# Broadcast means moved behind a slot's scores, first gated blocks and gates moved ahead, more idle products at the start

## The chip, the cores and the metric

The kernel runs on one core of one Trainium2 chip. The time is that of the device, in microseconds, for one execution; the median over runs counts. Five engines work side by side, each through its own instructions in order: TensorE (PE in the rows), VectorE (DVE), ScalarE (ACT), GpSimd (POOL), and SyncE (SP), which here only issues DMAs. They wait for each other by semaphores.

## The reference

Three layers, all in float32. Block-sparse attention over 2 batches, 8 heads, 768 positions of width 64; a mixture of 4 experts on the 1536 tokens of width 512; a gated MLP. Cut to what matters here:

```python
# attention, per batch and head; blocks of 32 positions, window 16
k_sum = k.reshape(nb, 32, D).max(1);  v_sum = v.reshape(nb, 32, D).mean(1)
scores = concat([where(|i-j| < 16, scale * q @ k.T, -1e9), scale * q @ k_sum.T + log(32)])
a = exp(scores - max);  a = a / (a.sum(-1) + 1e-9)
x = a @ concat([v, v_sum])
# experts
p = domain_probs / (domain_probs.sum(-1) + 1e-9)
x = sum(p[:, e:e+1] * (relu(x @ w1[e]) @ w2[e]) for e in range(4))
# last layer
h = x @ w_in;  out = (h * sigmoid(1.702 * h)) @ w_out
```

## The kernel before

**Precision.** Most products run with each float32 operand cut in two fp32r parts, high and low, as three matmuls (high by high, high by low, low by high). `split` makes such parts of a weight block: ACT casts the high part, DVE or POOL subtracts it from the raw block to get the low part. `hidden` and `low` do the same for activations.

**Attention in slots.** Two heads at a time (a head pair, `hp`, 4 per batch) and 4 windows of 64 queries make a group, named in the program by batch, head pair and first window (`010` is batch 0, pair 1, window 0). There are 24 groups: batch 0's twelve first, then batch 1's. The work is a pipeline written out by hand, one slot per group and a few behind them. Slot i holds, in the order in which each engine gets it: `att_a(i)`, then products of the first expert layer or idle products on TensorE, then `att_b(i)`.

- `att_a(i)`: `scores` of group i (16 small matmuls into PSUM bank 5, then on DVE the mask `s` and the row maximum `nm`); `normalise` of group i-1 (two short DVE instructions `sm`, a POOL product over `s`); `windows` of group i+2 (DVE and POOL copies into `kw`); the weight splits that the table `middle` names for the slot; in slots 0 to 3 and 12 to 15, where a new head pair begins, `fold_v` on POOL (half of a block sum of v), and in the slot behind each, `sums` on DVE (the other half, into `vsum`).
- `att_b(i)`: `transposes` of group i-2 (PE into bank 6, ACT copies to `aT`); `values` of group i-3 (PE into bank 7, tile `xo`; ACT casts to `xh`, and `low` later subtracts on DVE to `xl`); then `means` of group i-2; `exponentials` of group i on ACT; and what the table `after` names for the slot, mostly loads.
- `means(g)`: with the first group of a head pair, PE transposes `vsum` into a bank of its own name `pvs` (bank 4 in batch 0, bank 5 in batch 1) and ACT scales it into `vm`; for every group, POOL then copies `vm` to the last 24 rows of the group's v tile (`v_home` or `vw`). `values` of the next slot reads them.

**The start.** Loads are issued by SP in one order: keys, queries, v and weights of the first groups. 10 idle 128 by 128 products (`warm`, written by `spin`) run ahead of the first scores. Slots 0 to 3 have no other dense work; the list `SPIN` puts 0, 4, 4, 4 idle products into them behind the scores. Slots 4 to 7 hold `early(k)`: 12 products each, the part of head pair k of the first four hidden blocks (units 0 to 3, in banks 0 to 3).

**First expert layer.** A unit is 128 hidden channels by 256 or 512 tokens of batch 0. `first(i)` computes a unit's hidden block into a bank; `hidden(i)` makes it relu times gate on DVE (`gated`, tile `g`, which reads the broadcast gates `pb`), casts it on ACT, and puts the low part on the list `pending`, which `flush` empties on DVE. `second(i)` multiplies by the second weight into banks 0 to 3, the banks of units 0 to 3. So `second(0)` can write banks 2 and 3 only when the gated blocks 2 and 3 have been read. From slot 8 on, slots are interleaved with units: unit 4 has slots 8 and 9, unit 5 has 10 and 11, and so on (unit 8 has three, 16 to 18). In the kernel before, `hidden_blocks(0, 1)` stands behind slot 8 and `hidden_blocks(2, 3, 4)` behind slot 9, each with the low parts of the block before it in between, and `second(0)`, `second(1)` follow.

**Gates.** `gates_load` brings the probabilities (48 numbers per partition) after the loads of v; `gates`, behind slot 4, sums, adds, inverts and multiplies on DVE (four instructions), then stores them to DRAM; behind slot 5 `load_p(0, 0)` reads them back, broadcast to all partitions, as `pb`.

After the attention slots the rest of the program works through pairs of hidden blocks of the other experts and the last layer, 44 pairs, TensorE nearly always busy.

## Time and profile before

| | |
|---|---|
| median of 3 runs | 865.87 us (865.2 to 867.35) |
| the profiled execution's own time | 866.81 us |
| its span, first to last instruction | 865.0 us |
| mean granted TensorE clock | 0.993 |
| TensorE busy | 830.1 us, 96% |
| DVE, ACT, POOL busy | 602.0, 397.1, 479.6 us |
| slots 0 to 3 on TensorE | to 22.95 us (scores of slot 4) |
| slots 4 to 7 | 22.95 to 39.97 us |
| slots 8 to 18 | 39.97 to 96.97 us |

Times of instructions are counted from the span's start. A line of a list of waits tells how long an engine stood still before instructions of one line, how often, and whose work ended the wait. The granted clock is 1.00 where TensorE had its full 2.4 GHz and 0.50 where it had 1.2 GHz.

### The profile page before, as it was taken

What the parts mean: (1) busy time and instruction counts of PE and PEld (TensorE: products, weight loads), DVE (VectorE), ACT (ScalarE), POOL (GpSimd) and SP (SyncE); (2) the same over time, 40 slices, a digit from 0 to 9 for tenths busy, and PEclk for the clock granted to TensorE, in tenths of its full rate; (3) what the DMA queues carried; (4) which work ended last, traced back from release to release, by engine and by line L of the source; (5) the groups of instructions that cost most, each with busy time, mean ns of one, the idle gap of its engine ahead of it and who ended that gap; (6) DMA issues with size and microseconds to landing.
All of it is one profiled execution on the core that took longest, in us unless ns stands there. A gap on an engine that the chain in (4) does not pass through costs nothing.

```text
span 865.0 us, 13668 instructions
## 1 busy us (share of the span) xinstructions
PE 830.1 (96%) x5068; PEld 748.7 (87%) x5068; DVE 602.0 (70%) x899; ACT 397.1 (46%) x914; POOL 479.6 (55%) x416
## 2 busy tenths in 40 slices
PE   6978999999999999989999999999899999999998
PEld 5866778899999989889989998999788998998896
DVE  7677538879999884688788688897788753432332
ACT  4766742535444444233333334446556453434442
POOL 6657435656667674265564657867478642323221
PEclk9899999999999999999999999999999999999999
DMA  9853412366767536386776874223534627653422
GB/s 284 255 174 87 138 38 103 117 249 244 266 218 264 207 149 259 114 314 231 277 252 251 287 276 143 77 73 110 183 134 169 232 110 280 207 193 112 150 93 74
DMA packets 48371, 159.93 MB, mean 185 GB/s; under 512 B 5424, under 2 KB 8752, under 8 KB 43184
## 3 DMA queue, kind: packets, MB, share of 16 engines
q1 hardware_dynamic: 48304, 159.06, 53.3%
q8 instruction: 40, 0.66, 0.3%
q14 instruction: 27, 0.22, 0.1%
HBM read 110.78 MB, written 48.26 MB: 184 GB/s over the span
## 4 chain that ended last, share of the span: by engine, by line
PE 72%; DVE 14%; DMA 6%; issue 4%; ACT 2%; POOL 2%; SPq 0%; DVEq 0%; POOLq 0%; ACTq 0%
PE o L782 19%; PE Y L664 17%; PE o L807 13%; PE X L664 5%; PE h L387 3%; DVE S L547 3%; PE o L418 2%; DMA wA<-kept 2%; DVE hid L337 2%; PE sc L231 2%; DVE g L716 2%; PE xo L282 1%; DVE x L452 1%; DMA q<-kq 1%; DVE g L709 1%
## 5 line engine op out<-in xcount | busy, mean ns | idle before, releaser
L782 PE MATMUL o<-hid,wB 128*128 128x512 f32 x1344 | 261.3, 336 | 3.5 <-DVE y L799 2.3
L782 PEld LDWEIGHTS o<-hid,wB 128*128 128x128 f32 x1344 | 214.6, 188 | 25.4 <-DVE y L799 3.0
L576 POOL TENSOR_TENSOR wB<-rawB,wB 128x512 fp32r<-128x512 f32 x88 | 124.9, 1429 | 136.8 <-ACT wB L575 122.0
L807 PE MATMUL o<-wB,hid 128*128 128x512 f32 x576 | 147.8, 393 | 0.0
L711 ACT CAST hid<-g 128x384 fp32r<-128x384 f32 x176 | 90.7, 516 | 117.8 <-DVE g L701 82.4
L337 DVE TENSOR_TENSOR hid<-g,hid 128x384 fp32r<-128x384 f32 (+2 forms) x152 | 129.3, 858 | 19.1 <-ACT hid L711 13.6
L807 PEld LDWEIGHTS o<-wB,hid 128*128 128x128 f32 x576 | 106.9, 188 | 17.0
L552 POOL TENSOR_TENSOR wA<-S,wA 128x512 fp32r<-128x512 f32 x48 | 70.3, 1465 | 45.5 <-ACT wA L551 30.1
L701 DVE SCALAR_TENSOR_TENSOR g<-g,pb 128x384 f32<-128x384 f32 x84 | 83.3, 991 | 2.0
L552 POOL TENSOR_TENSOR wA<-rawA,wA 128x512 fp32r<-128x512 f32 (+1 forms) x48 | 59.7, 1243 | 42.0 <-ACT wA L551 36.4
L664 PE MATMUL Y<-xh,wA 128*128 128x384 f32 x224 | 66.2, 336 | 4.3 <-DMA wA<-kept 2.8
L664 PE MATMUL Y<-xt,wA 128*128 128x384 f32 x336 | 67.5, 335 | 1.7 <-ACT prq L724 1.5
L337 POOL TENSOR_TENSOR hid<-g,hid 128x384 fp32r<-128x384 f32 x40 | 45.6, 1141 | 30.0 <-ACT hid L711 30.0
L724 ACT COPY prq<-Y 128x384 f32<-128x384 f32 x44 | 21.2, 481 | 85.0 <-PE Y L664 68.7
L664 PEld LDWEIGHTS Y<-xt,wA 128*128 128x128 f32 x336 | 56.0, 188 | 4.7 <-ACT prq L724 2.0
L716 DVE TENSOR_TENSOR g<-X,prq 128x384 f32<-128x384 f32 x44 | 24.4, 555 | 43.0 <-PE X L664 40.3
L575 ACT CAST wB<-rawB 128x512 fp32r<-128x512 f32 x88 | 52.5, 619 | 1.4 <-DMA rawB<-wts 1.4
L261 POOL TENSOR_TENSOR s<-s,sm 128x480 f32<-128x480 f32 x24 | 28.3, 1180 | 40.9 <-DVE sm L260 38.5
L708 ACT ACTIVATE sg<-g 128x384 f32<-128x384 f32 x48 | 25.3, 527 | 55.9 <-DVE g L716 55.7
L709 DVE TENSOR_TENSOR g<-g,sg 128x384 f32<-128x384 f32 x48 | 34.2, 713 | 21.5 <-ACT sg L708 19.9
L664 PEld LDWEIGHTS Y<-xh,wA 128*128 128x128 f32 x224 | 41.2, 188 | 7.4 <-DVE arena L605 2.7
L615 POOL TENSOR_SCALAR arena<-arena 128x512 int32<-128x512 int32 x32 | 25.4, 792 | 39.6 <-DVE arena L611 39.6
(451 smaller groups left out, 1633.2 us busy)
## 6 DMA issues: line engine op xcount, KB each, us to landing
kept<-wA SPq DMA_DIRECT2D x20, 1792.0 KB, 6.7
wA<-kept SPq DMA_DIRECT2D x20, 1792.0 KB, 8.7
arena<-w SPq DMA_DIRECT2D x32, 512.0 KB, 4.9
rawB<-wts SPq DMA_DIRECT2D x28, 512.0 KB, 4.0
rawA<-wts SPq DMA_DIRECT2D x16, 512.0 KB, 7.8
w<-arena SPq DMA_DIRECT2D x32, 256.0 KB, 2.5
rawB<-w SPq DMA_DIRECT2D x16, 512.0 KB, 4.3
rawA<-w SPq DMA_DIRECT2D x8, 512.0 KB, 8.0
```

Source lines behind the costliest of these rows:

```text
L261: nc.gpsimd.tensor_tensor(out=s, in0=s, in1=sm.unsqueeze(2).to_broadcast([P, GW, KA]), op=ALU.mult)
L337: engine.tensor_tensor(out=hl, in0=g, in1=hh.bitcast(F32), op=ALU.subtract)
L552: nc.gpsimd.tensor_tensor(out=lo, in0=x, in1=hi.bitcast(F32), op=ALU.subtract)
L575: nc.scalar.copy(hi, rawB[j][:, f])
L576: nc.gpsimd.tensor_tensor(out=lo, in0=rawB[j][:, f], in1=hi.bitcast(F32), op=ALU.subtract)
L664: nc.tensor.matmul(ps[:, 0:HS], ws[w], xs[x][:, k], start=(fresh and k == 0 and m == 0), stop=(k == 1 and m == 2), skip_group_check=True,)
L701: nc.vector.scalar_tensor_tensor(out=g, in0=g, scalar=0.0, in1=pbs[ph, s][:, tok], op0=ALU.max, op1=ALU.mult)
L709: nc.vector.tensor_tensor(out=g, in0=c, in1=sg, op=ALU.mult)
L711: heads.append(lambda: nc.scalar.copy(hh, g))
L716: nc.vector.tensor_tensor(out=g, in0=ps, in1=x, op=ALU.add)
L782: nc.tensor.matmul(o, wB[j][:, w, f, c], tiles[f][:, x, t], start=fr, stop=last, skip_group_check=True,)
L807: nc.tensor.matmul(o, tiles[f][:, x, c], wB[j][:, w, f], start=(new and f == 1 and m == 0), stop=(old and f == 0 and m == 2),)
```

## The change

- **Means.** `means` of group i-2 moves from `att_b` behind `values` to `att_a` straight behind `scores`. The transpose of `vsum` no longer has a bank of its own name: it goes into columns 256 to 383 of the newest `xo` tile in bank 7 (in slot 2 into a fresh one). The next `values` takes a new tile in bank 7 and so comes after ACT's read of the transpose.
- **Gates.** Their load becomes the third load of the program. The sum is made on POOL in slot 0 (`gates_sum`, three short instructions); the inverse (DVE), the product (POOL) and the store come in slot 1, and the broadcast load in slot 4 in place of 5.
- **Gated blocks.** Blocks 0 and 1 come straight behind slot 7, blocks 2 and 3 straight behind slot 8, block 4 behind slot 9; the low parts come with the next slot's `flush`.
- **Idle products.** `SPIN` becomes 4, 8, 4, 4, and 4 more stand ahead of `values` in slots 2 and 3.
- **Split 2.** In slot 3 its low part moves from POOL to DVE, behind split 3.
- **Loads.** The queries of group 4 are issued ahead of the last v loads of batch 0.

```diff
--- before.py
+++ after.py
@@ -210,13 +210,17 @@
             axis=AX.X, op=ALU.add,
         )
 
+    xo = {}
+
     def means(g):
         b, hp, w0 = g
         if (b, hp) not in vms:
             vms[b, hp] = att.tile([P, P], F32, tag="vm", bufs=4, name=f"vm{b}{hp}")
-            ps = bank(5 if b else 4, f"pvs{b}{hp}")
-            nc.tensor.transpose(ps[0:KA, 0:P], vsum[hp % 2], ident)
-            nc.scalar.mul(vms[b, hp][KW:KA], ps[KW:KA, 0:P], 1.0 / BLK)
+            if "ps" not in xo:
+                xo["ps"] = bank(7, "xo")
+            ps = xo["ps"][:, GQ : GQ + P]
+            nc.tensor.transpose(ps[0:KA], vsum[hp % 2], ident)
+            nc.scalar.mul(vms[b, hp][KW:KA], ps[KW:KA], 1.0 / BLK)
         nc.gpsimd.tensor_copy(
             vs[g][KW:KA], vms[b, hp][KW:KA].unsqueeze(1).to_broadcast([NB, GW, P])
         )
@@ -276,7 +280,7 @@
         b, hp, w0 = g
         a = st.pop(g)
         v = vs.pop(g)
-        ps = bank(7, f"xo{b}{hp}{w0}")
+        ps = xo["ps"] = bank(7, f"xo{b}{hp}{w0}")
         for j in range(GW):
             for h in range(2):
                 nc.tensor.matmul(
@@ -308,13 +312,21 @@
     def gates_load():
         nc.sync.dma_start(out=dp, in_=dpT.rearrange("e (p c) -> p e c", c=NC))
 
+    ds = const.tile([P, NE // 2 + 1, NC], F32, name="ds")
+
+    def gates_sum():
+        two, one = ds[:, 0 : NE // 2], ds[:, NE // 2]
+        nc.gpsimd.tensor_tensor(out=two, in0=dp[:, 0 : NE // 2], in1=dp[:, NE // 2 :], op=ALU.add)
+        nc.gpsimd.tensor_tensor(out=one, in0=two[:, 0], in1=two[:, 1], op=ALU.add)
+        nc.gpsimd.tensor_scalar(
+            out=one, in0=one, scalar1=1.0, scalar2=1e-9, op0=ALU.mult, op1=ALU.add
+        )
+
     def gates():
-        ds = const.tile([P, NC], F32, name="ds")
-        nc.vector.tensor_reduce(out=ds, in_=dp.rearrange("p e c -> p c e"), axis=AX.X, op=ALU.add)
-        nc.vector.tensor_scalar(out=ds, in0=ds, scalar1=1e-9, scalar2=None, op0=ALU.add)
-        nc.vector.reciprocal(out=ds, in_=ds)
-        nc.vector.tensor_tensor(
-            out=dp, in0=dp, in1=ds.unsqueeze(1).to_broadcast([P, NE, NC]), op=ALU.mult
+        one = ds[:, NE // 2]
+        nc.vector.reciprocal(out=one, in_=one)
+        nc.gpsimd.tensor_tensor(
+            out=dp, in0=dp, in1=one.unsqueeze(1).to_broadcast([P, NE, NC]), op=ALU.mult
         )
         nc.sync.dma_start(out=pscr.rearrange("e (p c) -> p e c", c=NC), in_=dp)
 
@@ -842,6 +854,8 @@
     def att_a(i):
         if i < NG:
             scores(groups[i])
+        if 2 <= i < NG + 2:
+            means(groups[i - 2])
 
         if 1 <= i < HP - 1:
             maxima(*groups[i + 1][:2])
@@ -860,10 +874,9 @@
     def att_b(i):
         if 2 <= i < NG + 2:
             transposes(groups[i - 2])
+        spin(SPIN_MORE.get(i, 0))
         if 3 <= i < NG + 3:
             values(groups[i - 3])
-        if 2 <= i < NG + 2:
-            means(groups[i - 2])
         if i < NG:
             exponentials(groups[i])
         if 3 <= i < NG + 3:
@@ -876,7 +889,7 @@
     pool, dve = nc.gpsimd, nc.vector
     middle = {
         2: [lambda: split(0, A, pool), lambda: split(1, A, dve)],
-        3: [lambda: split(2, A, pool), lambda: split(3, A, dve)],
+        3: [lambda: split(3, A, dve), lambda: split(2, A, dve)],
         5: [lambda: split(0, C, pool)],
         6: [lambda: split(1, C, pool)],
         7: [lambda: split(4, A, dve)],
@@ -896,7 +909,9 @@
     def x_whole():
         xf[1] = slot("xf", [P, KC, S], F32, "x1")
 
-    after = {0: [x_parts], 4: [gates], 5: [lambda: load_p(0, 0)], 8: [x_whole]}
+    after = {
+        0: [x_parts, gates_sum], 1: [gates], 4: [lambda: load_p(0, 0)], 8: [x_whole],
+    }
 
     def later(i, *acts):
         after.setdefault(i, []).extend(acts)
@@ -919,6 +934,8 @@
     for hp in range(HP):
         load_k(0, hp)
         load_q(groups[hp])
+        if hp == 0:
+            gates_load()
         if hp in (1, 2):
             load_vt(0, hp - 1)
             load_v(groups[hp - 1])
@@ -928,10 +945,9 @@
     load_v(groups[2])
     load_w(2, A)
     load_w(3, A)
+    load_q(groups[4])
     load_vt(0, 3)
     load_v(groups[3])
-    gates_load()
-    load_q(groups[4])
     load_v(groups[4])
     load_q(groups[5])
 
@@ -947,7 +963,8 @@
         maxima(0, hp)
         windows(groups[hp])
     START = 4 + KC
-    SPIN = (0, 4, 4, 4)
+    SPIN = (4, 8, 4, 4)
+    SPIN_MORE = {2: 4, 3: 4}
     for i in range(START):
         att_a(i)
         if i < len(SPIN):
@@ -956,15 +973,8 @@
             early(i - len(SPIN))
         att_b(i)
 
-
-    def hidden_blocks(*blocks):
-        for i in blocks:
-            before = list(pending)
-            pending.clear()
-            hidden(i)
-            for act in before:
-                act()
-
+    for i in range(2):
+        hidden(i)
     sl = START
     LAST = NG + 3
     steps = []
@@ -994,12 +1004,13 @@
         n = SLOTS.get(i, 2)
         one_slot()
         if i == EARLY:
-            hidden_blocks(0, 1)
+            for k in range(2, EARLY):
+                hidden(k)
         first(i)
         for _ in range(n - 1):
             one_slot()
         if i == EARLY:
-            hidden_blocks(2, 3, 4)
+            hidden(i)
         if sl == LAST:
             flush()
         if i < EARLY + 2:
```

**PE, slot 3 to the head of slot 4, before** (`sc` scores, `at` transposes, `xo` values, `pvs` the transpose for the means, `h` a hidden block):

```order
L231 MATMUL sc030_279<-kw030_239,q030_129 64x120 x8
L943 MATMUL warm_146<-ident_68 128x128 x4
L269 MATMUL at010_308<-ident_68,s010_199 120x128 x4
L282 MATMUL xo000_315<-aT000_263,v_home0_91 64x64 x8
L218 MATMUL pvs01_326<-ident_68,vsum1_104 120x128
L231 MATMUL sc004_345<-kw004_245,q004_140 64x120 x8
L387 MATMUL h0_365<-xh0_186,w0A0_98 128x256
```

The same place after:

```order
L235 MATMUL sc030_298<-kw030_259,q030_131 64x120 x8
L222 MATMUL xo_253<-ident_68,vsum1_104 120x128
L959 MATMUL warm_147<-ident_68 128x128 x4
L273 MATMUL at010_331<-ident_68,s010_207 120x128 x4
L959 MATMUL warm_147<-ident_68 128x128 x4
L286 MATMUL xo000_342<-aT000_283,v_home0_91 64x64 x8
L235 MATMUL sc004_367<-kw004_265,q004_139 64x120 x8
L222 MATMUL xo000_342<-ident_68,vsum0_103 120x128
L399 MATMUL h0_391<-xh0_191,w0A0_98 128x256
```

The transpose of `vsum` now stands ahead of the slot's transposes and values instead of behind them, and four more idle products stand ahead of the values.

**DVE, from slot 8's last instructions to slot 10's mask, before** (`g` a gated block, `hid` its low part, `ks` block maxima, `xl` the low part of the attention's output):

```order
L168 TENSOR_TENSOR w0A1_99<-raw_b_97,w0A1_99 128x512
L337 TENSOR_TENSOR hid0_663<-g_667,hid0_663 128x256
L297 TENSOR_TENSOR xl0_187<-xo024_713,xh0_186 128x256
L187 TENSOR_REDUCE ks10_730<-k10_545 128x24
L331 SCALAR_TENSOR_TENSOR g_741<-h2_373,pb00_480 128x256
L331 SCALAR_TENSOR_TENSOR g_744<-h3_377,pb00_480 128x256
L337 TENSOR_TENSOR hid2_740<-g_741,hid2_740 128x256
L331 SCALAR_TENSOR_TENSOR g_749<-h4_671,pb00_480 128x256
L337 TENSOR_TENSOR hid2_740<-g_744,hid2_740 128x256
L239 SCALAR_TENSOR_TENSOR s028_790<-sc028_781,mask_73 128x480
```

The gated blocks 2 and 3 (`h2`, `h3`) after:

```order
L343 SCALAR_TENSOR_TENSOR g_629<-h1_395,pb00_430 128x256
L243 SCALAR_TENSOR_TENSOR s008_641<-sc008_632,mask_73 128x480
L248 TENSOR_REDUCE nm008_643<-s008_641 128x4
L263 TENSOR_SCALAR sm034_612<-sm034_612 128x4
L264 RECIPROCAL sm034_612<-sm034_612 128x4
L199 COPY kw028_649<-k02_124 128x4x96
L349 TENSOR_TENSOR hid0_625<-g_626,hid0_625 128x256
L349 TENSOR_TENSOR hid0_625<-g_629,hid0_625 128x256
L301 TENSOR_TENSOR xl0_192<-xo014_663,xh0_191 128x256
L343 SCALAR_TENSOR_TENSOR g_687<-h2_399,pb00_430 128x256
L343 SCALAR_TENSOR_TENSOR g_690<-h3_403,pb00_430 128x256
L243 SCALAR_TENSOR_TENSOR s018_715<-sc018_706,mask_73 128x480
```

The gated blocks 2 and 3 stood at the end of slot 9, behind its split, low part and block maxima; they now stand at the end of slot 8, ahead of slot 9's mask (`s018`), and blocks 0 and 1 ahead of slot 8's.

**POOL, slot 13, before** (`s` normalise, `kw` windows, `w0ex` a split, `vT` a fold, `vw` the copy of the means):

```order
L261 TENSOR_TENSOR s100_940<-s100_940,sm100_969 128x480
L200 COPY kw130_1016<-ks13_975 128x4x24
L168 TENSOR_TENSOR w0ex_102<-raw_b_97,w0ex_102 128x512
L181 TENSOR_TENSOR vT11_833<-vT11_833 128x24x16
L220 COPY vw038_831<-vm03_469 24x512
```

The same slot after:

```order
L224 COPY vw038_845<-vm03_449 24x512
L265 TENSOR_TENSOR s100_954<-s100_954,sm100_983 128x480
L200 COPY kw130_1031<-ks13_989 128x4x24
L168 TENSOR_TENSOR w0ex_102<-raw_b_97,w0ex_102 128x512
L181 TENSOR_TENSOR vT11_847<-vT11_847 128x24x16
```

The copy of the means went from the slot's last place on POOL to its first.

## Rows read from the trace of the kernel before

**Rows 1.** The page: span; busy time, share and instructions of each engine.

```profile
span 865.0 us, 13668 instructions
...
PE 830.1 (96%) x5068; PEld 748.7 (87%) x5068; DVE 602.0 (70%) x899; ACT 397.1 (46%) x914; POOL 479.6 (55%) x416
```

**Rows 2.** Stretches: length, busy PE, PEld, DVE, ACT, POOL, granted clock, DMA, GB/s.

```profile
0.00:28.00 28.00, 19.92 (x168) 17.49 (x170) 18.35 (x38) 12.16 (x42) 18.61 (x33) 0.88 0.98 298
...
40.00:73.00 33.00, 27.89 (x320) 24.14 (x320) 25.48 (x59) 22.51 (x84) 18.83 (x24) 0.95 0.60 182
73.00:96.00 23.00, 18.29 (x225) 14.71 (x222) 14.79 (x35) 14.64 (x53) 16.15 (x21) 1.00 0.31 90
96.00:126.00 30.00, 29.99 (x291) 23.77 (x292) 13.39 (x31) 17.66 (x68) 13.12 (x19) 1.00 0.27 86
126.00:160.00 34.00, 32.27 (x173) 26.70 (x170) 24.99 (x27) 12.52 (x23) 14.36 (x9) 1.00 0.20 70
```

**Rows 3.** Waits of PE, 0 to 160 us: total, times, longest.

```profile
PE xo L282 <- POOL vw L220: 5.9, 8, 1.9
PE o L418 <- DVE g L331: 3.0, 1, 3.0
...
PE xo L282 <- POOL v_home L220: 2.3, 1, 2.3
...
PE sc L231 <- DMA q<-kq: 0.7, 1, 0.7
```

**Rows 4.** Two single microseconds, columns as in rows 2.

```profile
22.00:23.00 1.00, 0.30 (x3) 0.08 (x3) 0.42 (x1) 0.95 (x5) 1.00 (x3) 0.50 1.04 363
...
53.00:54.00 1.00, 1.00 (x6) 1.00 (x6) 0.00 (x0) 0.01 (x1) 0.00 (x0) 0.50 0.00 0
```

**Rows 5.** The chain that ended last: start, us, what, instructions.

```profile
22.95 1.87 PE sc L231 x16
24.82 2.72 PE h L387 x12
...
28.85 0.97 PE sc L231 x16
29.81 1.63 PE h L387 x12
...
50.75 3.91 PE o L418 x18
...
61.66 3.07 PE o L418 x24
```

**Rows 6.** PE in order of time, slot 1: four idle products.

```profile
9.21 1.16 PE L943 MATMUL warm<-ident 128*128 128x128 f32 x8
```

**Rows 7.** DVE in order of time: start, us, what, idle before and releaser.

```profile
16.05 0.68 DVE L168 TENSOR_TENSOR w0A<-raw_acc,w0A 128x512 fp32r<-128x512 f32 x1
...
20.12 1.10 DVE L168 TENSOR_TENSOR w0A<-raw_a,w0A 128x512 fp32r<-128x512 f32 x1
...
22.30 0.42 DVE L297 TENSOR_TENSOR xl<-xo,xh 128x256 fp32r<-128x256 f32 x1 [0.62 <-ACT xh L290]
...
50.28 0.74 DVE L331 SCALAR_TENSOR_TENSOR g<-h,pb 128x256 f32<-128x256 f32 x2
```

**Rows 8.** DMA issues, 0 to 60 us: KB each, median us to landing.

```profile
k<-kq SPq DMA_DIRECT2D x8, 400.0 KB, 6.2
...
dp<-dpT SPq DMA_DIRECT2D x1, 24.0 KB, 7.2
```

**Rows 9.** POOL in order of time, slot 13.

```profile
71.40 1.52 POOL L261 TENSOR_TENSOR s<-s,sm 128x480 f32<-128x480 f32 x1 [0.96 <-DVE sm L260]
...
73.29 1.27 POOL L168 TENSOR_TENSOR w0ex<-raw_b,w0ex 128x512 fp32r<-128x512 f32 x1
74.53 0.99 POOL L181 TENSOR_TENSOR vT<-vT 128x384 f32<-128x384 f32 x1
75.58 0.61 POOL L220 COPY vw<-vm 24x512 f32<-24x512 f32 x1
```

## Prediction

> **What bounds the kernel now.** I read the page first, then the stretches, then who ended PE's waits, and last the chain and single microseconds where the clock fell. PE is busy 830.1 of the 865.0 us span [rows 1], so the reader should see a program bound by TensorE almost everywhere, and ask where the missing 35 us lie. The stretches show it: PE stands still 28.00 - 19.92 = 8.08 us in the first 28 us, 33.00 - 27.89 = 5.11 us from 40 to 73 us, 23.00 - 18.29 = 4.71 us from 73 to 96 us, and 30.00 - 29.99 = 0.01 us from 96 to 126 us [rows 2]. From 96 us on TensorE itself is the bound, and so whatever is won ahead of 96 us arrives at the end undiminished, unless a later stage has a bound of its own. The list of waits names what held PE there: 5.9 us in eight waits of the attention values for POOL's copy of the means, 3.0 us in one wait of `second(0)` for gated blocks on DVE, 2.3 us for the first copy of the means, 0.7 us for the queries of group 4 [rows 3]. Besides, the granted clock was 0.50, the 1.2 GHz level, at 22 us and again at 53 us, each time behind such a wait [rows 4]; there PE is busy and yet slow. All edits of the change lie in these stretches.
>
> **First part, slots 0 to 4.** Two things set the end of this part at present: PE's wait for the copy of the means, and the slow clock behind it. The 16 scores of slot 4 took 1.87 us where the same 16 took 0.97 a slot later, and the 12 early products 2.72 where they then took 1.63 [rows 5].
>
> The change moves POOL's first copy of the means ahead of a normalise, a split and a fold, so the wait of 2.3 us before the first values [rows 3] goes. What is late next? On PE, slot 3 now has four idle products more in front of the values. Four take 1.16 us [rows 6]. That fills half of the 2.3 us, so the first values come about 1.1 us sooner. All 16 added products are 4 x 1.16 = 4.6 us at most, in a stretch with 8.08 us of PE idle time [rows 2]; they are hidden by PE's waits for keys' copies, mask and means, and would cost up to 4.6 us if that cover were gone. On DVE, the low part `xl` of slot 3 began at 22.30 us after 0.62 us of waiting for ACT [rows 7]; without that wait it could have begun at 21.68. The low part of split 2 now goes ahead of it on DVE. It takes between 0.68 and 1.10 us, the two splits of its kind on DVE [rows 7]. So `xl` begins at 22.4 to 22.8, ends 0.42 us later, and the early products, which need it, begin at 22.8 to 23.2 in place of 24.82: 1.6 to 2.0 us won. If the clock holds, the 12 early products also take 1.63 in place of 2.72, another 1.09. Together 2.7 to 3.1; I take 2.9, in the middle. The transpose for the means now stands between the scores and the early products and waits for `vsum`, which DVE makes just ahead of that same `xl`; so it adds a wait that is over before the next one. The queries of group 4 are issued two loads sooner, which takes their 0.7 us wait off the path.
>
> The gates: their load becomes SP's third, and the keys and queries of the second group queue behind it. Its 24 KB took 7.2 us to land in a full queue, keys of 400 KB took 6.2 [rows 8]. By bytes it costs 24/400 of 6.2 = 0.4 us of the queue; at the upper end I put the difference of 1.0 us. A gain is excluded here, since the same load merely moves forward. I take 0.3, near the price by bytes, as the scores of the second group wait for the mask on DVE as well. The three sums on POOL stand behind the first fold, where POOL then waits for DVE; the store stands on SP behind loads that are throttled by earlier landings, so SP does not stand still for POOL's product, and behind it only weights are queued. Should POOL be late there, the weight loads wait with it, and splits have a slot of slack. The product and sums leave DVE in slot 4, and load `pb` a slot sooner. Net for the part: 2.9 - 0.3 = 2.6 us; the bounds are -1.0 (the clock falls all the same and the load costs its upper price) and 3.1.
>
> The Trainium skill (DMA: Bandwidth & Descriptors, Specifications) says that transfers below 512 bytes do not reach line rate. This load consists of 48-byte pieces, and by that rule it is nearer the upper price, which would make the sum 0.7 us smaller.
>
> **Second part, slots 8 to 13.** PE idles 5.11 us here [rows 2], of which 3.0 are the wait of `second(0)` [rows 3]: banks 2 and 3 are free only once DVE has read the blocks at 50.28 us [rows 7], at the very end of slot 9's DVE work. After the change blocks 2 and 3 stand ahead of slot 9's mask, a whole slot of DVE work sooner, so the wait goes. The slow clock behind it goes too: 18 products took 3.91 us, 24 later ones 3.07, so 18 are worth 2.30 and 1.61 us are won [rows 5]. The other 2.1 us are waits for the copy of the means, dealt with below. All of it: 5.11 + 1.61 = 6.72.
>
> What is late next is DVE. It is busy 25.48 of the 33 us [rows 2]; with 33 - 6.72 = 26.28 us left it would be busy 97% of the time, so the cover is almost used up. Its own work does not grow, it only comes sooner. The price of a collision with POOL I read from the two splits, 1.10 - 0.68 = 0.42 us [rows 7]. I leave one for every second of the six slots, 1.26 us, and take 6.72 - 1.3 = 5.4. The lower bound is the 3.0 of the one wait alone, the upper one 6.7. ACT, at 22.51 us, would be at 82 to 86% and is not the bound.
>
> The Trainium skill (GPSIMD Engine Reference, Specifications) has POOL share its SBUF interface with DVE instructions that read two SBUF operands. Most of DVE's low parts do. By that rule every slot has its collision, 6 x 0.42 = 2.5 us, and the sum would be 1.2 us smaller.
>
> **Third part, slots 14 to 18.** PE idles 4.71 us [rows 2], nearly all before values, behind POOL. In slot 13 POOL's normalise starts at 71.40 only when DVE is through with the slot's mask and maxima; then come copies, a split of 1.27, a fold of 0.99 and last the means, from 75.58 for 0.61 us [rows 9]. The next values wait for that. With the means in first place, POOL has them done before it waits for DVE. What is late next is the normalise, now up to 0.61 us later in POOL's slot, which the transposes of the slot after need; and POOL itself, busy 16.15 us of what becomes about 18.7, or 86%. With a new head pair POOL also stands behind ACT's scaling of the transpose, with normalise, split and fold queued behind. I leave 0.4 us for that and take 4.3. If the 0.61 came through in all five slots, 3.0 of the 4.7 would be lost: the bounds are 1.7 and 4.7.
>
> **The sum.** 2.6 + 5.4 + 4.3 = 12.3 us. The profiled execution took 866.81 us, its span 865.0, so I expect 854.5 for such an execution. It stands 0.94 above the median of 865.87; against the median I forecast 853.6. The bounds of the terms add up to gains of 3.7 to 14.5.
>
> **Rivals.**
> *The clock falls all the same at the start.* For it: it was down at 22 us [rows 4] behind idle stretches that the idle products only partly fill. Against it: with them PE has little idle time left from 12 to 20 us. The 0.90 of the scores and 1.09 of the early products are then paid again, 2.0 us: 855.6.
> *DVE becomes the bound in slots 8 to 13.* For it, the 97%. Against it, DVE stood still for 7.5 of the 33 us [rows 2], and its work merely comes sooner. Only the lower bound of 3.0 is then won there, 2.4 less: 856.0.
> *Slower: the transpose for the means holds up PE.* It stands now at the head of the slot, with the transposes, values and dense products behind it, and needs POOL's fold and DVE's sum of the slots before, in eight slots. If each time it comes a split and a fold too early, 1.27 + 0.99 = 2.26 us [rows 9], 18.1 us are lost and 12.3 won: 871.7. From 12.3/8 = 1.5 us a slot on the kernel is slower than before. Against it: in the early slots the sum ends about when the scores do, and a fold is a slot ahead.
> *Nothing arrives.* The gain ahead of 96 us is given back where the expert pairs begin, from 126 to 160 us, with DVE at 24.99 of 34 us. Against it: PE is busy there 32.27 us [rows 2], and the work there starts from PE's last attention slots, so it moves with them. It would give 865.9.
>
> **How the numbers follow.** The forecast has 0.62, the clock 0.15, DVE 0.14, the slower case 0.04, nothing 0.05. The predicted time is 853.6. The range goes from 851.0, all terms near their upper bounds (a gain of 14.5 and half a microsecond of the runs' own spread), to 858.8, where two rivals of the first two kinds come together (2.0 + 2.4 lost: 858.0) with the same margin and a little of the third part's lower bound. Faster by over 0.3%, 2.6 us, is what a measurement of this kernel can tell from no change: the forecast and the first two rivals, 0.91; within it 0.05; slower 0.04.
>
> **What would show it.** In the changed profile: the scores of slot 4 near 21 to 22 us, the early products behind them in about 1.6 us with a granted clock of 1.00 throughout; no wait of `o` for `g` at 44 to 50 us; no 0.50 in the clock's rows there; the waits of the values for POOL's copy gone or under 1 us in total; the dense stretch that began at 96 us [rows 2] beginning at about 84. I would be wrong if the clock's row falls somewhere new, if the list of waits names the transpose for the means waiting for DVE's sum, or if PE's idle time appears behind 126 us.

## The result, and the profile after

| | before | after |
|---|---|---|
| median | 865.54 us (865.18 to 867.35) | 855.37 us (854.47 to 858.16) |
| ratio to before, 95% interval | | 0.988 [0.9857, 0.9904] |
| the profiled execution's own time | 866.81 us | 855.06 us |
| its span | 865.0 us | 853.3 us |
| mean granted clock | 0.993 | 0.999 |

The change makes the kernel 1.2% faster, 10.2 us by the medians. The time lies in the forecast range, 1.8 us above the 853.6 that were forecast.

The page of the kernel after: span, engines, and the granted clock in 40 slices.

```profile
span 853.3 us, 13736 instructions
...
PE 827.9 (97%) x5100; PEld 748.4 (88%) x5100; DVE 604.6 (71%) x897; ACT 395.2 (46%) x914; POOL 481.3 (56%) x419
...
PEclk9999999999999999999999999999999999999999
```

The engines have the same work as in [rows 1], but for the added idle products. Of the 11.7 us by which the span is shorter, 9.5 are standstill of TensorE (865.0 - 830.1 = 34.9 us before, 853.3 - 827.9 = 25.4 after); it is also busy 2.2 us less, at a higher granted clock. The stretches of the same work as in [rows 2], in the same columns (length, busy PE, PEld, DVE, ACT, POOL, granted clock, DMA, GB/s), at their new times:

```profile
0.00:38.00 38.00, 31.94 (x360) 28.82 (x360) 27.47 (x59) 21.95 (x78) 26.52 (x47) 1.00 0.97 295
38.00:64.00 26.00, 25.60 (x317) 22.34 (x314) 24.68 (x57) 21.18 (x79) 18.30 (x23) 1.00 0.66 197
64.00:85.00 21.00, 19.51 (x235) 16.05 (x234) 17.73 (x37) 15.97 (x62) 17.98 (x24) 1.00 0.38 113
85.00:115.00 30.00, 30.00 (x296) 23.77 (x296) 13.38 (x31) 17.68 (x65) 11.79 (x16) 1.00 0.27 80
115.00:149.00 34.00, 32.29 (x161) 26.83 (x160) 25.91 (x28) 12.18 (x22) 15.34 (x10) 1.00 0.20 70
```

Slots 8 to 13 were 33 us with 5.11 of PE idle time; they are 26 with 0.40. Slots 14 to 18 were 23 with 4.71; they are 21 with 1.49. The dense stretches behind (fourth and fifth line) are as they were: what is won ahead of them arrives.

PE's waits in the first 160 us of the kernel after (total, times, longest):

```profile
PE xo L222 <- DVE xl L301: 1.7, 2, 1.4
PE Y L676 <- ACT prq L736: 1.5, 1, 1.5
PE warm L959 <- POOL ident masks.py:199: 1.4, 1, 1.4
PE at L273 <- POOL s L265: 1.3, 2, 1.0
PE sc L235 <- POOL kw L200: 1.3, 2, 1.0
PE xo L222 <- DVE vsum L207: 1.2, 1, 1.2
```

All four waits of [rows 3] are gone: values for POOL's copies (5.9 and 2.3 us), `o` for `g` (3.0), scores for queries (0.7). In their place stand waits of the moved transpose (L222) for DVE, 2.9 us in three; the transposes' waits for POOL's normalise are 1.3 us, and were 0.4 before.

**Where the time came from.** I read the start of the first score of a slot from PE's rows in order of time. For the first part I count from the start of DVE's maxima of the second head pair (`ks`), which waits for a DMA; its place varies from one execution to the next, and so it is taken out. Each ratio is to runs of the kernel before that were taken together with the variant. One of the twelve runs of `only_idle` took 918.69 us at a granted clock of 0.847 and is not in its ratio.

| kernel | ratio [95%] | `ks` | `ks` to slot 8 | slot 8 to 14 | slot 14 to 19 |
|---|---|---|---|---|---|
| before | 1 | 5.74 | 34.23 | 32.76 | 24.24 |
| after | 0.988 [0.9857, 0.9904] | 7.03 | 31.07 | 26.16 | 20.88 |
| only_means | 0.9938 [0.9926, 0.9951] | 7.41 | 30.39 | 31.17 | 20.84 |
| only_blocks | 0.995 [0.9932, 0.9968] | 6.08 | 31.23 | 28.78 | 24.21 |
| only_idle | 0.9989 [0.9973, 1.0005] | 6.03 | 32.98 | 32.76 | 24.22 |
| all_but_idle | 0.9881 [0.9866, 0.9896] | 6.64 | 31.06 | 26.16 | 20.86 |
| all_but_gates | 0.9858 [0.9841, 0.9875] | 6.82 | 31.06 | 26.15 | 20.84 |
| gates_load_later | 0.9914 [0.9885, 0.9944] | 6.29 | 35.47 | 26.15 | 20.87 |
| own_bank | one time, 857.62 us | 7.83 | 31.60 | 26.15 | 22.75 |
| split_on_pool | one time, 853.84 us | 6.19 | 30.38 | 26.16 | 20.86 |
| changed_again (after, repeated) | 0.9876 [0.9861, 0.9891] | 6.14 | 31.08 | 26.17 | 20.84 |
| split_pool_timed | 0.9868 [0.9851, 0.9884] | 6.87 | 30.41 | 26.16 | 20.86 |
| split_pool_old_gates | 0.9851 [0.9832, 0.987] | 6.29 | 30.40 | 26.18 | 20.85 |
| split_pool_old_idle | 0.9865 [0.9848, 0.9883] | 7.14 | 30.41 | 26.17 | 20.86 |

In the two profiles slot 8 starts 39.97 - 38.10 = 1.87 us sooner, slots 8 to 13 are 6.60 shorter and 14 to 18 are 3.36 shorter: 11.83 in all, against 11.7 of span. The last two columns repeat within 0.05 us between kernels with the same instructions there. `ks` does not, and from `ks` to slot 8 the kernel before and `only_blocks`, which have the same instructions there, are 3.00 us apart.

### The profile page after: what moved, and what is told of

Its sections match the earlier page's. It is cut to its first block, busy times and chain, and to the rows that moved or that the text cites. A ratio compares the mean times of both kernels' runs of the same rounds, so it can differ in the third digit from the quotient of the medians.

```text
span 853.3 us, 13736 instructions
## 1 busy us (share of the span) xinstructions
PE 827.9 (97%) x5100; PEld 748.4 (88%) x5100; DVE 604.6 (71%) x897; ACT 395.2 (46%) x914; POOL 481.3 (56%) x419
## 4 chain that ended last, share of the span: by engine, by line
PE 75%; DVE 16%; issue 3%; DMA 2%; ACT 2%; POOL 1%; SPq 0%; DVEq 0%; ACTq 0%; POOLq 0%
PE o L794 21%; PE Y L676 18%; PE o L819 14%; PE X L676 5%; PE h L399 3%; DVE S L559 3%; DVE hid L349 2%; PE o L430 2%; PE sc L235 2%; DVE g L728 1%; DMA arena<-w 1%; PE xo L286 1%; DVE x L464 1%; PE at L273 1%; DVE g L721 1%
## 5 line engine op out<-in xcount | busy, mean ns | idle before, releaser
L736 ACT COPY prq<-Y 128x384 f32<-128x384 f32 x44 | 21.1, 480 | 86.2 <-PE Y L676 69.2
L751 ACT COPY prq<-Y 128x384 f32<-128x384 f32 x44 | 21.1, 479 | 54.2 <-PE Y L676 54.0
```

## The experiments

The theory is that of the prediction: the means and the gated blocks shorten slots 8 to 18, and the idle products, with the sooner means, keep the clock up at the start. The rivals for the start are that the idle products do nothing there, or that an early load costs what they win.

**One part alone.** `only_means`: the kernel before with the diff's edits of `means` and the tile `xo`, `att_a` and `att_b`.

```diff
+        if 2 <= i < NG + 2:
+            means(groups[i - 2])
...
-        if 2 <= i < NG + 2:
-            means(groups[i - 2])
```

> The kernel before with the move of the means alone. Theory (the parts act in separate places): POOL's copy no longer holds up the values, so the waits of the values for POOL, 5.9 + 2.3 us before, go. From slot 8 to 13 about 2.1 us are won, from slot 14 to 18 about 3.4 as in the changed kernel; the wait of 3.0 us of second(0) for the gated blocks and the slow clock at 53 us stay. At the start the clock still falls or not, open: 0 to 2 us. Time 5.5 to 7.5 us under the kernel before, some 859. Rival (the means only pay together with the earlier gated blocks, since DVE then becomes free for the slots behind): under 3 us won.

It is 0.62% faster. The whole gain of slots 14 to 18 is there (20.84), and 1.59 us of that of slots 8 to 13, where 2.1 were expected. PE's waits in its first 100 us show what then stands in front:

```profile
PE o L422 <- DVE g L335: 3.7, 1, 3.7
PE sc L235 <- POOL kw L200: 2.9, 2, 1.7
PE sc L235 <- DVE s L243: 2.7, 1, 2.7
```

With the means out of the way, the wait of `o` for `g` grew from 3.0 [rows 3] to 3.7 us: PE arrives sooner at the same late block.

`only_blocks`: the kernel before with the gated blocks moved.

```diff
+    for i in range(2):
+        hidden(i)
...
-            hidden_blocks(0, 1)
+            for k in range(2, EARLY):
+                hidden(k)
...
-            hidden_blocks(2, 3, 4)
+            hidden(i)
```

> The kernel before with the gated blocks alone put sooner: blocks 0 and 1 behind slot 7, 2 and 3 behind slot 8, 4 behind slot 9; gates and their loads as before. Theory: the wait of 3.0 us goes and with it the 0.50 of the clock's rows behind it, worth 1.6: 4.6 us won, some 861, all of it between slot 8 and slot 10. Rival (the broadcast gates are not there in time without their earlier load): DVE waits for the load at the first gated block, and less than 2 us are won.

It is 0.5% faster, with 3.98 us in slots 8 to 13 and nothing behind. DVE's waits in its first 100 us have none for the broadcast gates: that rival fell. Singly the two edits give 1.59 + 3.98 = 5.57 us there, together 6.60: each alone leaves the other's wait as the next limit. Here it is the wait of slot 9's values for POOL's copy, which was 0.48 us in the kernel before:

```profile
44.26 0.69 PE L282 MATMUL xo<-aT,vw 120*64 120x64 f32 x16 [1.25 <-POOL vw L220]
```

Up to slot 7 this kernel has exactly the instructions of the kernel before. Yet the clock fell elsewhere. Two stretches of `only_blocks` (columns as above):

```profile
14.00:16.00 2.00, 1.77 (x10) 1.37 (x11) 1.97 (x6) 1.35 (x3) 0.52 (x2) 0.50 1.07 309
...
22.00:24.00 2.00, 2.00 (x25) 1.84 (x26) 1.29 (x3) 1.79 (x9) 2.00 (x4) 1.00 1.07 373
```

The granted clock was 0.50 at 14 us and 1.00 at 22 us, where [rows 4] have 0.50. Slot 8 came 31.23 us behind `ks` and not 34.23. PE's scores of slot 4, in the kernel before and in `only_blocks`, tell where the 3.00 us arose:

```profile
22.95 1.87 PE L231 MATMUL sc<-kw,q 64*64 64x120 f32 x16 [0.70 <-DMA q<-kq]
```

```profile
21.93 1.04 PE L231 MATMUL sc<-kw,q 64*64 64x120 f32 x16 [0.22 <-DMA q<-kq]
```

They start 17.21 and 15.85 us behind `ks`, in both when the load of their queries has landed; that is 1.36 us. Slot 4 itself, from its scores to those of slot 5, took 5.83 us at the low clock and 4.19 at full clock, another 1.64. So 3.0 us of the start of the kernel before, as profiled, belong to that execution and not to the program: 1.64 to the fall of the clock in slot 4, the rest to when its queries landed.

**The idle products.** `only_idle` is the kernel before with the new `SPIN` and `SPIN_MORE`; `all_but_idle` is the kernel after with the old ones:

```diff
-    SPIN = (4, 8, 4, 4)
-    SPIN_MORE = {2: 4, 3: 4}
+    SPIN = (0, 4, 4, 4)
+    SPIN_MORE = {}
```

> The kernel before with the added idle products alone. Theory (the idle products keep the clock up at the start): granted clock 1.00 from 20 to 27 us in place of 0.50, the 12 early products of slot 4 in about 1.6 us, 1.5 to 2.5 us won, some 863.5. Rival (what brings the clock down is the wait of PE for the first copy of the means, which stays here, shortened by the products in front of it): the clock still falls and the time is that of the kernel before or up to 1 us longer.

> The changed kernel with the idle products of the kernel before (0, 4, 4, 4 and none ahead of the values). Theory (idle products keep the clock up): granted clock 0.50 somewhere from 18 to 28 us, 1.5 to 2.5 us more than the changed kernel. Rival (the moved means alone took away the idle time that brings the clock down): clock 1.00 throughout, and the time of the changed kernel or up to 1 us less, since the values of slot 3 start sooner.

Alone they give 0.11%, with an interval that holds no change. Without them the change is worth the same (0.9881 against 0.988). First stretches of `only_idle`, then of `all_but_idle`:

```profile
22.00:24.00 2.00, 1.62 (x17) 1.35 (x17) 0.64 (x2) 1.33 (x8) 2.00 (x2) 0.67 1.05 364
24.00:26.00 2.00, 2.00 (x10) 2.00 (x10) 1.89 (x6) 0.00 (x0) 0.92 (x3) 0.50 1.03 371
```

```profile
18.00:20.00 2.00, 1.58 (x8) 1.61 (x9) 1.97 (x4) 1.12 (x3) 2.00 (x2) 0.62 1.06 309
20.00:22.00 2.00, 2.00 (x21) 1.66 (x22) 1.97 (x4) 0.86 (x2) 1.86 (x4) 0.52 1.07 318
```

The clock fell in spite of them in the one, and in the other it fell at no cost: slot 8 comes 31.06 us behind `ks`, as in the kernel after. There DVE is busy 1.97 of each 2.00 us, and PE, after the slow stretch, still has to wait for it (0.71 us, where the kernel after has 1.41):

```profile
23.93 0.33 PE L222 MATMUL xo<-ident,vsum 128*120 128x128 f32 x1 [0.71 <-DVE xl L301]
```

**The gates.** `all_but_gates` is the kernel after with load, sum, product and broadcast of the gates as before.

```diff
-        0: [x_parts, gates_sum], 1: [gates], 4: [lambda: load_p(0, 0)], 8: [x_whole],
+        0: [x_parts], 4: [gates], 5: [lambda: load_p(0, 0)], 8: [x_whole],
...
-        if hp == 0:
-            gates_load()
...
+    gates_load()
```

> The changed kernel with the gates as they were: load behind the v loads, four DVE instructions and the store behind slot 4, broadcast load behind slot 5. Theory (the early load of 24 KB in small pieces holds up the second group's keys): DVE's maxima of the second group start near 5.8 us in place of 7.03, the scores of slots 1 to 3 come 0.6 to 0.7 us sooner, as in the kernel before, and slot 8 begins up to 0.7 us sooner if the broadcast gates are there in time. Rival (the gates had to come sooner for the earlier gated blocks): DVE waits for the broadcast load at the first gated block behind slot 7, and slot 9 or 10 begins more than 1 us later than in the changed kernel.

It loses nothing. Its `ks` starts at 6.82 us and not near 5.8, so the theory's reason, the second keys held up by the early load, is not borne out by this profile. The broadcast gates are in time for the blocks behind slot 7 all the same, as this row of DVE, in order of time, shows; it has no wait behind it:

```profile
38.74 0.75 DVE L335 SCALAR_TENSOR_TENSOR g<-h,pb 128x256 f32<-128x256 f32 x2
```

`gates_load_later` is the kernel after with only the load moved behind the keys and queries of the fourth pair:

```diff
-        if hp == 0:
+        if hp == HP - 1:
```

> The changed kernel with one edit: the load of the probabilities is issued behind the fourth group's keys and queries in place of the first group's. Theory (only its place in front of the second group's keys costs): scores of slots 1 to 3 some 0.6 us sooner than in the changed kernel, and everything behind too unless the sums on POOL, which then wait for a later landing at about 14 us, hold up the windows and the normalise queued behind them: POOL then stands still in slot 0, and the scores of slot 2 come 1 to 3 us later. Rival (the delay of the second group's keys comes from elsewhere): scores of slot 1 at 8.9 us as in the changed kernel.

It gives back 3 us of the gain by the ratios. POOL in order of time, and a line of PE's waits:

```profile
14.35 0.23 POOL L319 TENSOR_TENSOR ds<-dp 128x24 f32<-128x24 f32 x1 [5.06 <-DMA dp<-dpT]
...
15.22 0.26 POOL L200 COPY kw<-ks 128x96 f32<-128x96 f32 x1
```

```profile
PE sc L235 <- POOL kw L200: 3.9, 1, 3.9
```

POOL works in order. While its first sum stood 5.06 us for the load, the windows of the next group were queued behind it, and the scores of slot 2 waited 3.9 us for those. Slot 8 comes 4.4 us later behind `ks`. So whoever makes the sums on POOL in slot 0 must load early; with the sums left in slot 4 neither is needed.

**The tile of the transpose.** `own_bank` is the kernel after with the transpose for the means back in its own bank name. It tests the mechanism of the slower rival: a transpose at the head of a slot that has to wait.

```diff
-            if "ps" not in xo:
-                xo["ps"] = bank(7, "xo")
-            ps = xo["ps"][:, GQ : GQ + P]
-            nc.tensor.transpose(ps[0:KA], vsum[hp % 2], ident)
+            ps = bank(5 if b else 4, f"pvs{b}{hp}")
+            nc.tensor.transpose(ps[0:KA, 0:P], vsum[hp % 2], ident)
```

> The changed kernel with the transposes of the block sums in the banks of the kernel before: bank 4 in batch 0, the bank of the scores, 5, in batch 1, at their new place. Theory (a transpose at the head of a slot passes its wait on to the whole slot): in slots 14 to 17 the transpose now waits for DVE's mask to read the scores of the same slot, some 1 us each, and the stretch from slot 14 to slot 19, 20.9 us in the changed kernel, grows by 3 to 5 us; in slots 2 to 5 the wait for the low part of the slot before, 1.4 us at slot 4, goes, but the early products wait for that low part anyway, so nothing is won there. Rival (slack in the slots hides it): under 1 us more.

PE's waits in its first 100 us:

```profile
PE pvs L220 <- DVE s L241: 3.2, 4, 0.9
PE pvs L220 <- DVE vsum L207: 2.4, 2, 1.2
```

Bank 5 is also that of the scores, so the transpose right behind them waits for DVE's read of them, at most 0.9 us at a time. Slots 14 to 18 are 22.75 - 20.88 = 1.87 us longer, less than the theory's 3 to 5. The four waits of together 3.2 us lie in slots 14 to 17; the kernel after has two others in slots 14 to 18, of 0.33 and 1.01 us (below), which `own_bank` has not. 3.2 - 1.34 is the 1.87 but for 0.01: the waits at the head of a slot are passed on whole, and as PE comes later to slot 18, that slot's normalise is done in time. From `ks` to slot 8 it is 0.53 us longer, so nothing is won there, as expected.

**The split.** `split_on_pool` and `split_pool_timed` are one kernel: the kernel after with split 2 back on POOL.

```diff
-        3: [lambda: split(3, A, dve), lambda: split(2, A, dve)],
+        3: [lambda: split(2, A, pool), lambda: split(3, A, dve)],
```

> The changed kernel with the splits of slot 3 as before: split 2 with its low part on POOL, then split 3 on DVE. Theory (what sets the start of the early products is DVE's work of slot 3 ahead of the low part): the low part begins about 0.7 us sooner than its 23.86 us, the early products about as much, and slot 8 begins 0.5 to 0.7 us sooner than 38.10. Rival (the early products need the low part of split 2, which POOL has only behind its normalise and windows): PE waits for POOL in the middle of the early products, and slot 8 begins at 38.1 us or later.

> The changed kernel with slot 3's splits as before (split 2 on POOL), now timed. Theory (DVE's slot 3 sets the start of the early products): counted from DVE's maxima of the second group, slot 8 begins 0.7 us sooner than in the changed kernel (30.4 in place of 31.1 us behind them), and the time is 0.5 to 1 us under that of the changed kernel on the same chip. Rival (the single look was 1.5 us better because its loads landed sooner): slot 8 begins 31.1 us behind the maxima, time as the changed kernel.

> The changed kernel as it is, once more, so that the three variants beside it can be compared on one chip. Both theories expect 854 to 857 us and the stage lengths of its first profile: 26.2 us from slot 8 to 14, 20.9 from slot 14 to 19. What differs from execution to execution (start of DVE's maxima of the second group, 5.7 to 7.8 us so far; low stretches of the granted clock at the start; waits for kept weights behind 350 us) shows how much of a single profile is the program's.

DVE in order of time, `ks` and slots 2 and 3, first the kernel after, then `split_on_pool`:

```profile
7.03 0.95 DVE L187 TENSOR_REDUCE ks<-k 128x24 f32<-128x768 f32 x1 [1.69 <-DMA k<-kq]
...
16.72 1.48 DVE L168 TENSOR_TENSOR w0A<-raw_acc,w0A 128x512 fp32r<-128x512 f32 x1
...
21.33 1.48 DVE L168 TENSOR_TENSOR w0A<-raw_a,w0A 128x512 fp32r<-128x512 f32 x1
22.73 0.74 DVE L168 TENSOR_TENSOR w0A<-raw_acc,w0A 128x512 fp32r<-128x512 f32 x1
...
23.86 0.41 DVE L301 TENSOR_TENSOR xl<-xo,xh 128x256 fp32r<-128x256 f32 x1
```

```profile
6.19 0.95 DVE L187 TENSOR_REDUCE ks<-k 128x24 f32<-128x768 f32 x1 [1.06 <-DMA k<-kq]
...
20.48 1.48 DVE L168 TENSOR_TENSOR w0A<-raw_a,w0A 128x512 fp32r<-128x512 f32 x1
...
22.35 0.41 DVE L301 TENSOR_TENSOR xl<-xo,xh 128x256 fp32r<-128x256 f32 x1
```

`xl`, for which the early products wait, starts 23.86 - 7.03 = 16.83 us behind `ks` after the change, and 22.35 - 6.19 = 16.16 with the split on POOL. Slot 8 gains the same 0.67: 31.07 and 31.08 became 30.38 to 30.41 in all four profiles of such kernels with the split on POOL. In `split_on_pool` slot 8 came at 36.57 us, 1.53 sooner than 38.10; the rest of that is a sooner `ks`. PE has no wait for POOL among the early products there. Measured together, 855.34 and 854.33 us are the medians of after and of this kernel, 1.0 us apart; their intervals overlap, so the time alone does not show it, the rows do.

**Put together.** `split_pool_old_gates` adds the edits of `all_but_gates` to that kernel, `split_pool_old_idle` those of `all_but_idle`.

> Split 2 on POOL and, besides, the gates as in the kernel before (load behind the v loads, all on DVE behind slot 4, broadcast load behind slot 5). Theory (the gates' early place is worth nothing, since the broadcast gates land ahead of the first gated block in either case): no wait of DVE for the gates behind slot 7, time within 1 us of the kernel with split 2 on POOL alone. Rival (they are needed with the start 0.7 us sooner): DVE waits for the broadcast load behind slot 7, slot 9 begins 1 us or more later.

> Split 2 on POOL and, besides, the idle products of the kernel before. Theory (with the means moved, a low clock in slots 2 and 3 falls into time in which TensorE waits for DVE anyway): time within 1 us of the kernel with split 2 on POOL alone, even where the granted clock shows 0.50 between 14 and 22 us. Rival (with DVE quicker, TensorE is closer to being the bound and the low clock costs): 1.5 to 2.5 us more in runs where it falls, a median 1 us or more above.

The first has the lowest median, 852.89 us, and the second, 854.04, is level with `split_pool_timed`: no worth of the idle products shows here either. In its profile the clock did not fall at the start, so it does not try the theory's claim of a fall without cost. `split_pool_old_gates` beats the kernel before, 0.9851, and has a lower median than the kernel after (855.34 in the same comparison), with intervals that overlap a little (up to 0.987 against from 0.9861). Both pairs with and without the early gates lean the same way, by 0.0018 to 0.0022 and by 0.0017, and neither settles it.

## Why the prediction was right, and where it was not

The profile's gain of 11.83 us lies near the 12.3 of the sum, and in part by luck: the first and third part gave 0.73 and 0.94 us less than forecast, the second 1.20 more.

**Second part: right, and the reserve was not needed.** I forecast 5.4 from 6.72 minus 1.3 for collisions of DVE with POOL; 6.60 came. DVE is busy 24.68 of 26.00 us there, 95%, near the 97% worked out, and PE 25.60: the cover held, and the rival in which DVE becomes the bound fell. The Trainium skill (GPSIMD Engine Reference, Specifications) has POOL share its SBUF interface with VectorE instructions of two SBUF inputs, and by it the prediction had 1.2 us less. The trace agrees that there are such collisions, and the measurement decides that slots 8 to 13 lost hardly anything to them. In DVE's rows of these slots two low parts took 1.61 us together, where one later took 0.42, beside POOL's normalise, and PE did not wait for them:

```profile
46.26 1.61 DVE L349 TENSOR_TENSOR hid<-g,hid 128x256 fp32r<-128x256 f32 x2
...
51.10 0.42 DVE L349 TENSOR_TENSOR hid<-g,hid 128x256 fp32r<-128x256 f32 x1
```

```profile
45.66 1.52 POOL L265 TENSOR_TENSOR s<-s,sm 128x480 f32<-128x480 f32 x1 [0.68 <-ACT xh L294]
```

Where collisions did cost is slots 2 and 3 (the split, below).

**Third part: the mechanism right, the size too large.** 4.3 were forecast, within 1.7 to 4.7; 3.36 came. The step that was too generous is to take the 4.71 us of idle time as waits before values, nearly all. In PE's rows of the kernel before, 1.89 + 0.24 + 1.41 + 0.23 = 3.77 us are that. 0.51 more is a wait of slot 18's scores for ACT's read of the transpose, which then had the scores' bank; it is gone after the change. The last 0.42 is a wait for POOL's normalise, and the sooner means do not take that away:

```profile
92.40 1.04 PE L231 MATMUL sc<-kw,q 64*64 64x120 f32 x16 [0.51 <-ACT vm L219]
93.86 0.65 PE L269 MATMUL at<-ident,s 128*120 128x128 f32 x4 [0.42 <-POOL s L261]
```

So 3.77 + 0.51 = 4.28 us could be won. The term that was too small is the 0.4 left for the normalise and ACT. The rows of PE and of POOL of the kernel after show what was given back:

```profile
65.62 0.33 PE L222 MATMUL xo<-ident,vsum 128*120 128x128 f32 x1 [0.33 <-DVE xl L301]
...
82.31 0.65 PE L273 MATMUL at<-ident,s 128*120 128x128 f32 x4 [1.01 <-POOL s L265]
```

```profile
80.71 1.54 POOL L265 TENSOR_TENSOR s<-s,sm 128x480 f32<-128x480 f32 x1 [0.39 <-DVE sm L264]
```

1.01 us is the transposes of slot 18 waiting for that normalise, which ends at 82.25 and had itself waited for DVE. It is the same wait as the 0.42, longer by 0.59, near the 0.61 by which I had the normalise later. I had named this wait for up to five slots; it came in one. The other 0.33 us is new: the transpose shares its tile with the attention output, and waits until DVE has read that output's low part, though it writes other columns. 4.28 - 0.59 - 0.33 is the 3.36 that came. `only_means` has the same 20.84, so all of it, gain and rest, belongs to the edits of the means and their tile.

**First part: the sum near, the reason wrong.** 2.6 were forecast, 1.87 came in the profiles. Counted from `ks` it is 34.23 - 31.07 = 3.16, where I had 2.9. The low part `xl` came 16.83 us behind `ks`, and the early products 24.40 - 7.03 = 17.37; the forecast's 22.4 to 22.8 and 22.8 to 23.2, less the 5.74 of `ks` before, are 16.66 to 17.06 and 17.06 to 17.46. PE's rows in order of time show the place:

```profile
21.87 1.04 PE L235 MATMUL sc<-kw,q 64*64 64x120 f32 x16
24.32 0.32 PE L222 MATMUL xo<-ident,vsum 128*120 128x128 f32 x1 [1.41 <-DVE xl L301]
24.40 0.37 PE L399 MATMUL h<-xh,w0A 128*128 128x256 f32 x1
```

The scores of slot 4 come at 21.87, as forecast, at full clock (1.04 us, against 1.87 in [rows 5]), and then PE stands 1.41 us for `xl`. So much was right. Three steps were not. Besides, the lower bound of this part, -1.0, does not follow from its own prices: 2.9 less 2.0 for the clock and 1.0 for the load is -0.1.

*The clock.* I took it that sooner means and idle products keep it up, and put 2 us on that. In the profile of after it was at 1.00 in every stretch shown above, as forecast. But the runs showed that where it falls is the execution's and not the program's (`only_blocks`), that idle products don't prevent a fall, in the kernel before (`only_idle`) or in the changed one (`own_bank`, row below), and that in one profile without them the fall cost nothing in the changed kernel (`all_but_idle`). The rival in which the clock falls all the same had its premise right for the executions of `all_but_idle` and `own_bank`, and its price of 2.0 us wrong for the first. Against the 31.23 of `only_blocks`, the change won 0.16 us at the start and not 3.16. `only_means`, with the split still on POOL and the clock at 1.00 from 10 to 28 us, came to 30.39: profile against profile, the sooner means are worth 0.84 us, and the split on DVE (next) took 0.67 of them back. What the sooner load of the queries is worth no run shows by itself.

A stretch of `own_bank`, columns as above:

```profile
12.00:14.00 2.00, 2.00 (x12) 1.78 (x12) 1.97 (x6) 1.62 (x8) 0.47 (x2) 0.50 1.05 370
```

*The split on DVE.* Its price was about right, 0.67 us against 0.68 to 1.10; what I left out is that it need not be paid. With it, `xl` starts 16.83 us behind `ks`, later than the 22.30 - 5.74 = 16.56 of the kernel before [rows 7]: it used up all that the sooner means had won on DVE. The two splits ahead of it, too, took 1.48 us each, beside POOL's normalise and copies, where [rows 7] have 0.68 and 1.10.

*The load of the gates.* I had 0.3 us for it, 1.0 at most. In the profiles `ks` starts at 7.03 with it and at 5.74 without, 1.29 later; but over all kernels it is 6.14 to 7.83 with the early load and 5.74 to 7.41 without. The spread covers any such price, so it stays open. The Trainium skill (DMA: Bandwidth & Descriptors, Specifications) says that pieces below 512 bytes miss line rate, and by it the load would be dearer; the row shows 4.3 us to its landing, against 4.5 for keys of 400 KB, which tells of its own delay and not of what it costs the others. No run here shows that.

```profile
k<-kq SPq DMA_DIRECT2D x8, 400.0 KB, 4.5
...
dp<-dpT SPq DMA_DIRECT2D x1, 24.0 KB, 4.3
```

**Why the median gained less than the profile.** Slots 8 to 18 are 6.60 + 3.36 = 9.96 us shorter, alike in every profile of this code. The ratios of after make 10.4 and 10.7 us of 865.54. That leaves 0.4 to 0.8 us for the start, with intervals of 1.3 to 2 us either way, and not the 2.6 of the forecast; `only_means` (5.4 by its ratio, 4.99 by its two columns) and `only_blocks` (4.3 and 3.98) leave the same 0.3 to 0.4. That the start is worth little in the median fits the clock's fall there being an accident of the profiled execution; it is worked out from ratios, and not shown by itself.

**The rivals on the other side.** *The transpose for the means holds up PE:* it was in place, with 2.9 us of waits in three. I had put 2.26 us a slot on it, in eight slots; the longest waits were 1.2 and 1.4 us, both at the start. The first was for DVE's sum, which I had named as a sign of being wrong; it stands in the list of waits, and the forecast time came all the same, so the sign was too strict. At the second, the early products behind it needed the same `xl`. `own_bank` shows that the mechanism is real. *Nothing arrives:* PE is busy 32.29 of the 34 us where the expert pairs begin, as in [rows 2]; it fell.

## What to carry to other kernels

Before a gain is expected from a slow stretch of one profile, profile the same instructions again: where the clock falls and when a load lands can belong to the execution. When work is moved between engines to shorten one queue, price the neighbours that it collides with and not only the instruction, and see whose result the next engine waits for. Work that is put ahead in an in-order queue must have its data there by then, or all that stands behind it waits too, as the sums of the gates showed.

## What was not expected of the hardware

- With the same instructions up to slot 7, the granted clock was 0.50 at 22 us in one execution and at 14 us in another; slot 4 took 5.83 us in the one and 4.19 in the other.
- A collision of DVE and POOL is paid by the one or the other. In the kernel before, DVE's split at 16.05 took 0.68 us [rows 7]; in the kernel after the same one took 1.48. POOL's normalise beside it took 1.55 us before and 1.01 after. POOL in order of time, before and then after:

```profile
16.04 1.55 POOL L261 TENSOR_TENSOR s<-s,sm 128x480 f32<-128x480 f32 x1 [0.23 <-ACT aT L271]
```

```profile
16.64 1.01 POOL L265 TENSOR_TENSOR s<-s,sm 128x480 f32<-128x480 f32 x1 [0.17 <-DVE sm L264]
```

- A TensorE transpose into columns of a PSUM tile waited for DVE's read of other columns of the same tile, 1.41 and 0.33 us in the profile of after. Whether the chip or the program's semaphores ask for that was not tried.
